# Bucketed attention and a mixture of experts on one core: a new order for VectorE's finishing steps, GpSimd's early gathers and the first weight splits

## The chip, the cores and the metric

One core of a Trainium2 chip runs the whole program. TensorE (PE) does the matmuls, VectorE (DVE), ScalarE (ACT) and GpSimd (POOL) the elementwise work, SyncE (SP) issues most DMAs. Each engine takes its own instructions in one fixed order and waits on semaphores for the others. The metric is the device time in microseconds.

## The reference, cut to what matters

```
mask   = q_bucket[:, :, :, None] == k_bucket[:, :, None, :]     # 6 sign bits of q @ proj, k @ proj
scores = where(mask, q @ k.T / 8, -1e9);  attn = softmax(scores);  x = attn @ v    # 4 x 8 heads x 768 x 64
x      = x.transpose(0, 2, 1, 3).reshape(3072, 512)
logits = x @ w_gate + modality_bias[modality_id]
e_idx  = argmax(logits);  gate_w = softmax(logits)[e_idx]
out[e_idx == e] = gate_w * (relu(x @ w1[e]) @ w2[e])            # 8 experts, 512 -> 1024 -> 512
```

## The kernel before, in words

**Attention.** The 32 heads are worked off as 16 pairs of heads, i = 0 to 15, four pairs to a batch of 768 tokens. A pair has six steps, one for each block of 128 keys. In a step TensorE makes the scores of all queries against the block (`score`, L278 and L279), ScalarE takes the exponential (pb, L291 and L296), TensorE multiplies by the values (`weigh`, L316), and the exponentials are summed (sp, L299) for the row sums: on GpSimd, two adds a step, except that in pair 15 the second head's adds are on VectorE, which leaves GpSimd five adds there. The exponentials lie in a ring of four buffers, freed only when both the value matmuls and the adds have read them. Between the score parts TensorE makes the row maxima of pair i+1 (`maxp`, reduced by VectorE from PSUM at L224 and L230, result mx) and turns, signs and patterns of pair i+2: `signs` gives bits (VectorE, L195), the bits times a pattern matrix (TensorE, L205) give the bucket rows of the operands, `maxp_back` puts the maxima into a_0g, a_1g and lone (VectorE, L249 and L250).

PSUM has two buffers for the maxima (psm) and two for transposes, patterns and the small products (psx).

**Finishing a batch.** Once a batch's four pairs are through, its outputs are finished beside the next batch's pairs, one generator step at a time (`finish`): row sums gs, reciprocals rin (L369 to L373), gate logits gl and lg (L377, L380), and `route`, which on VectorE makes the softmax and the argmax (l, rd, rw, oh, L567 to L580), the rank of each token in its expert (rk, run, pos, L595 to L601), and scatters records into a table with indirect DMAs on GpSimd (L605). For the last batches `finish_last` first runs `early_slots`: once two batches are routed it gives the two early expert slots their experts (L616 to L655, some 20 small VectorE operations on 128 x 8 to 128 x 96 elements: sg, enb, sc, ecu, ecux, sel, selx, selr, eslot, selw, early), and `early_tables` loads their token lists.

**Experts.** Two early slots, then the late ones, run as gathers of 512 token rows (xg, L766, four indirect DMAs on GpSimd), transposes, and matmuls in three products of high and low halves (L795 to L797, L839 to L841). Weights come in as raw and are split: ScalarE casts the high half (L749), the low half is a subtraction (L751) on VectorE or GpSimd: `pool = n % 2 == 1 if n < CFG["pn"]`.

**What sets the order.** TensorE and SyncE run in the order in which the code issues. For attention that is PLAN, one string for each of the six steps: S a score part, M a part of the maxima, T a piece for pair i+2, A values, B `maxp_back`, Q the row sums of the pair before, and the lower letters and G, F, E steps of finishing, which FIN gives to the pairs of a batch. VectorE, ScalarE and GpSimd are ordered by a scheduler when the program is built, from dependences and estimated costs; `tc.issue_after(ins)` puts what is issued in it behind the instruction ins on the same engine, an order only, with no semaphore.

## Time and profile before

| | |
|---|---|
| median of 3 runs | 827.99 us (827.86 to 829.27) |
| the profiled execution | 831.15 us, its span 829.4 us |
| mean granted TensorE clock | 0.974 |
| busy: TensorE, VectorE, ScalarE, GpSimd | 775.1, 490.8, 435.4, 448.4 us |

The profile is one execution, taken by the hardware profiler; all times in it count from the span's start. L195 is line 195 of the kernel before. In the changed file the same lines stand one to five lines lower from L23 on, some in `route` by other amounts. A timeline row gives start and length of an instruction, then in square brackets how long its engine was idle before it and what ended that wait. [...]

### The profile page before, as it was taken

To read this page: it belongs to the slowest core of one execution; us is meant where nothing else is said; L and a number is where in the kernel's file an instruction comes from. 1 tells how busy PE (TensorE), PEld (TensorE's weight loads), DVE (VectorE), ACT (ScalarE), POOL (GpSimd) and SP (SyncE) were. 2 spreads that over 40 slices of the span, in tenths; PEclk is the share of its full clock that TensorE was granted. 3 is DMA by queue.
4 is the path that set the end of the run, shared out by engine and by line. 5 is a ranking of instruction groups with operands and counts; after the bars stand their busy time and mean duration, and the time that the engine had idled before them with its cause. 6 is when DMAs were issued, how large, how long until landed. Compare 5 with 4: busy or idle time off the path is not lost. (4 is left out here: it accounts for less than half of the span.)

```text
span 829.4 us, 12179 instructions
## 1 busy us (share of the span) xinstructions
PE 775.1 (93%) x4252; PEld 548.5 (66%) x4252; DVE 490.8 (59%) x856; ACT 435.4 (52%) x788; POOL 448.4 (54%) x330
## 2 busy tenths in 40 slices
PE   5799999999999999999989898999999999999992
PEld 3556656565665665666556655888888888888882
DVE  5766767668886669776786656664344244643420
ACT  4477767666666666647655455333243335534340
POOL 5197788768769966859877976043220203302011
PEclk9699999999999999999998999999999999999996
DMA  9673446435545632743443327345543436733411
GB/s 205 141 169 97 96 115 152 104 70 134 148 101 134 152 94 74 178 129 63 115 115 95 123 82 185 131 98 187 161 125 107 146 103 204 268 102 118 124 49 36
DMA packets 105159, 104.27 MB, mean 126 GB/s; under 512 B 59389, under 2 KB 80509, under 8 KB 105088
## 3 DMA queue, kind: packets, MB, share of 16 engines
q1 hardware_dynamic: 98992, 88.61, 41.6%
q0 software_dynamic: 4928, 13.14, 4.5%
q10 hardware_dynamic: 1168, 1.64, 0.6%
q8 instruction: 36, 0.59, 0.3%
q14 instruction: 35, 0.29, 0.1%
HBM read 59.88 MB, written 13.33 MB: 88 GB/s over the span
## 5 line engine op out<-in xcount | busy, mean ns | idle before, releaser
L299 POOL TENSOR_TENSOR sp<-sp,pb 128x768 f32<-128x768 f32 x124 | 226.7, 1860 | 7.1 <-ACT pb L296 7.0
L291 ACT ACTIVATE pb<-pss 128x512 f32<-128x512 f32 x192 | 114.0, 602 | 101.0 <-PE pss L279 93.4
L224 DVE TENSOR_REDUCE mx<-psm 128x1 f32<-128x512 f32 x192 | 130.2, 686 | 30.3 <-PE psm L222 28.2
L316 PE MATMUL psu<-pb,vt 128*64 128x512 f32 (+1 forms) x768 | 134.2, 492 | 0.0
L751 DVE TENSOR_TENSOR w<-raw,w 128x1024 fp32r<-128x1024 f32 x60 | 75.5, 1260 | 96.8 <-ACT w L749 91.6
L749 ACT CAST w<-raw 128x1024 fp32r<-128x1024 f32 x64 | 67.0, 1049 | 75.8 <-PE yps L841 65.7
L316 PEld LDWEIGHTS psu<-pb,vt 128*64 128x64 f32 x768 | 51.0, 136 | 69.1 <-issue 58.8
L278 PE MATMUL pss<-a_0g 128*128 128x512 f32 x192 | 80.7, 420 | 4.9 <-ACT pb L291 4.2
L299 POOL TENSOR_TENSOR sp<-pb,pb 128x768 f32<-128x768 f32 x31 | 57.1, 1862 | 48.0 <-ACT pb L296 47.8
L839 PE MATMUL yps<-w,hl 128*128 128x512 f32 x208 | 82.6, 397 | 0.0
L841 PE MATMUL yps<-w,hh 128*128 128x512 f32 x208 | 81.3, 391 | 0.0
L840 PE MATMUL yps<-w,hh 128*128 128x512 f32 x208 | 81.0, 389 | 0.0
L795 PE MATMUL hps<-xh,w 128*128 128x512 f32 x192 | 76.7, 399 | 3.0 <-DVE hl L802 3.0
L797 PE MATMUL hps<-xh,w 128*128 128x512 f32 x192 | 76.1, 396 | 0.0
L796 PE MATMUL hps<-xl,w 128*128 128x512 f32 x192 | 76.1, 396 | 0.0
L278 PE MATMUL pss<-a_1g 128*128 128x512 f32 x192 | 70.7, 368 | 3.7 <-ACT pb L296 3.7
L230 DVE TENSOR_REDUCE mx<-psm 128x2 f32<-128x512 f32 x96 | 66.1, 689 | 9.6 <-PE psm L228 8.7
L766 POOL DMA_INDIRECT xg<-x_d,tb x18 | 22.1, 1227 | 91.8 <-DMA tb<-tab 87.5
L849 POOL DMA_INDIRECT out<-y,tb x18 | 19.1, 1059 | 95.2 <-ACT y L848 44.9
L801 ACT ACTIVATE hh<-hps 128x512 fp32r<-128x512 f32 x48 | 28.6, 597 | 79.5 <-PE hps L797 79.5
L279 PE MATMUL pss<-b_0g 128*128 128x512 f32 x192 | 66.3, 345 | 0.0
L279 PE MATMUL pss<-b_1g 128*128 128x512 f32 x192 | 66.2, 345 | 0.0
(210 smaller groups left out, 1484.1 us busy)
## 6 DMA issues: line engine op xcount, KB each, us to landing
raw<-moe_w SPq DMA_DIRECT2D x64, 512.0 KB
qk<-q SPq DMA_DIRECT2D x32, 192.0 KB
qk<-k SPq DMA_DIRECT2D x32, 192.0 KB
vt<-v SPq DMA_DIRECT2D x16, 384.0 KB
a_0g<-hx SPq DMA_DIRECT2D x30, 192.0 KB
a_1g<-hx SPq DMA_DIRECT2D x30, 192.0 KB
b_1g<-hx SPq DMA_DIRECT2D x30, 192.0 KB
b_0g<-hx SPq DMA_DIRECT2D x30, 192.0 KB
```

The lines of the kernel that those rows point to most:

```text
L224: nc.vector.tensor_reduce(out=mx[:, qt + j, 1 - h, 0:1], in_=mp, axis=AX.X, op=ALU.max)
L278: nc.tensor.matmul(out, t["s1"][h][:, ks], t["m1"][h][:, cs], start=True, stop=False)
L279: nc.tensor.matmul(out, t["s2"][h][:, ks], t["m2"][h][:, cs], start=False, stop=True)
L291: nc.scalar.activation(pb[:, h, 0:MAIN], sp, AF.Exp, scale=0.125)
L299: add = (nc.vector if h and i in CFG["spd"] else nc.gpsimd).tensor_tensor(out=t["sp"][:, h], in0=(t["pb"][0] if kt == 1 else t["sp"])[:, h ...
L316: nc.tensor.matmul(t["u"][part][64 * h:64 * h + 64, 0:w], t["v"][:, h, kt], t["pb"][kt][:, h, COLS[part]], start=False, stop=(kt == NT - 1 ...
L795: nc.tensor.matmul(hps, lo[:, c, fs], xh[:, c], start=(c == 0), stop=False)
L796: nc.tensor.matmul(hps, hi[:, c, fs], xl[:, c], start=False, stop=False)
L797: nc.tensor.matmul(hps, hi[:, c, fs], xh[:, c], start=False, stop=(c == 3))
L839: nc.tensor.matmul(yps[g], hl[fc][:, gs], hi[:, fb], start=(fc == 0), stop=False)
L840: nc.tensor.matmul(yps[g], hh[fc][:, gs], lo[:, fb], start=False, stop=False)
L841: nc.tensor.matmul(yps[g], hh[fc][:, gs], hi[:, fb], start=False, stop=(fc == 7))
```

## The change

Five edits. (1) The newest maximum reduction on VectorE is remembered, and every step of finishing is issued behind it. (2) In `route` the ranks rk and run move ahead of the softmax sum, with one more yield, and `finish_last` skips four places at step 12 instead of 11. (3) One G of PLAN moves from the last step of a pair to the third: two copies of gate values move earlier on TensorE in pairs 4 and 8. (4) The gathers of the early slots are issued on GpSimd behind named adds, counted from the last add of all. (5) `pn` goes from 8 to 0, so that all first splits are on VectorE.

```diff
+GAT = ((-5, -4, -4, -3), (-1, -1, -1, -1))
 PLAN = (
...
-    "SMTSMSMlEfxyk",
+    "SMTSMSMlGEfxyk",
...
-    "SMTSMTSMBAAFGBGFfFfggehkk",
+    "SMTSMTSMBAAFBGFfFfggehkk",
...
                     with tc.high_priority(offset=CFG["hm"]):
-                        nc.vector.tensor_reduce(out=mx[:, qt + j, 1 - h, 0:1], in_=mp, axis=AX.X, op=ALU.max)
+                        newest[:] = [nc.vector.tensor_reduce(out=mx[:, qt + j, 1 - h, 0:1], in_=mp, axis=AX.X, op=ALU.max).ins]
...
                     if add.ins.engine == mybir.EngineType.Pool:
                         latest[:] = [add.ins]
+                        adds.append(add.ins)
...
-            if n == 11:
+            if n == 12:
                 for _ in range(4):
                     yield
...
                     elif c in FIN[i >= NPR - 4][i % 4]:
-                        next(fins, None)
+                        with tc.issue_after(newest[0]):
+                            next(fins, None)
...
+        rk = wk.tile([P, NT, E], F32, name="rk")
+        nc.vector.tensor_tensor(out=rk, in0=pp[:, 0:NT * E].rearrange("p (t e) -> p t e", e=E), in1=run[b % 2].unsqueeze(1).broadcast_to([P, NT, E]), op=ALU.add)
+        nc.vector.tensor_tensor(out=run[(b + 1) % 2], in0=run[b % 2], in1=pp[:, 64:64 + E], op=ALU.add)
+        yield
         rec = recs[:, b]
         sm = wk.tile([P, NT], F32, name="rsum")
...
         for g in range(n):
-            nc.gpsimd.indirect_dma_start(out=xg[:, g], out_offset=None, in_=src, in_offset=bass.IndirectOffsetOnAxis(ap=at[:, g, 0:1], axis=0))
+            with tc.issue_after(adds[GAT[s[1]][g]]) if s[0] == "e" else nullcontext():
+                nc.gpsimd.indirect_dma_start(out=xg[:, g], out_offset=None, in_=src, in_offset=bass.IndirectOffsetOnAxis(ap=at[:, g, 0:1], axis=0))
```

Where this moves instructions is seen in the order that the build gives to each engine. The first place is VectorE in pair 12, before: maxima (mx), the sign operand b_1g, then bits.

```order
L224 TENSOR_REDUCE mx<-psm 128x1
L230 TENSOR_REDUCE mx<-psm 128x2
L224 TENSOR_REDUCE mx<-psm 128x1
L165 TENSOR_TENSOR b_1g_117<-psx,hx 128x512
L224 TENSOR_REDUCE mx<-psm 128x1
L230 TENSOR_REDUCE mx<-psm 128x2
L238 TENSOR_REDUCE m_4358<-mx 128x8
L195 TENSOR_SCALAR bits_164<-psx 128x384
```

The same place after the change; sg and enb stand some rows earlier among the maxima.

```order
L627 TENSOR_TENSOR sc_4386<-klow,enb 128x64
L239 TENSOR_REDUCE m_4362<-mx 128x8
L669 MEMSET ezero 128x8
L629 TENSOR_REDUCE ecu<-sc_4386 128x8
L631 TENSOR_TENSOR ecux<-ecu,enb 128x8
L638 TENSOR_TENSOR sel_4394<-ecu,kslot 128x16
L640 TENSOR_TENSOR selx_4396<-ecux,kslot 128x16
L641 TENSOR_TENSOR sel_4394<-sel_4394,selx_4396 128x16
L642 TENSOR_TENSOR selx_4396<-sel_4394,ke_66 128x16
L644 TENSOR_REDUCE selr_4400<-selx_4396 128x2
L645 CAST eslot<-selr_4400 128x2
L196 TENSOR_SCALAR bits_164<-psx 128x384
```

The first half of the early slots' chain now stands between the maxima of pair 12 and bits; before it stood in pair 11 ahead of gs (L339). Its second half, selw to selx, now stands behind the first lone of pair 12, ahead of the second a_0g.

The second place is VectorE in pair 13, before: the gate logits and the argmax of the third batch, then bits.

```order
L377 TENSOR_TENSOR gl<-gn,rin 128x384
L238 TENSOR_REDUCE m_4719<-mx 128x8
L380 TENSOR_REDUCE lg<-gl 128x48
L567 TENSOR_TENSOR l<-lg,bias 128x48
L569 TENSOR_REDUCE rm<-l 128x6
L571 TENSOR_TENSOR rd<-l,rm 128x48
L576 SCALAR_TENSOR_TENSOR rw<-rd,ke_66 128x48
L578 TENSOR_REDUCE rwm<-rw 128x6
L590 TENSOR_REDUCE rsum<-rex 128x6
L580 TENSOR_TENSOR oh<-rw,rwm 128x48
L591 TENSOR_SCALAR rsum<-rsum 128x6
L195 TENSOR_SCALAR bits_165<-psx 128x384
```

After the change, from the last maxima ahead of bits on.

```order
L231 TENSOR_REDUCE mx<-psm 128x2
L239 TENSOR_REDUCE m_4719<-mx 128x8
L196 TENSOR_SCALAR bits_165<-psx 128x384
L225 TENSOR_REDUCE mx<-psm 128x1 x2
L231 TENSOR_REDUCE mx<-psm 128x2
L374 SCALAR_TENSOR_TENSOR rin<-rin 128x48
L225 TENSOR_REDUCE mx<-psm 128x1
L375 RECIPROCAL rin<-rin 128x48
L225 TENSOR_REDUCE mx<-psm 128x1
L231 TENSOR_REDUCE mx<-psm 128x2
L250 SCALAR_TENSOR_TENSOR a_0g_114<-psx,a_0g_114 64x512
```

The chain from gl on is gone from ahead of bits: rin is among the maxima behind bits, gl comes behind the first lone, lg behind the second, and l to oh stand among the first maxima of pair 14.

The third place is GpSimd in the last pair, before: row scatters (L605), adds (L299), then the first splits (L751). Ahead of it, before the first add of pair 14, stood the eight gathers (L766).

```order
L605 DMA tab<-recs,posi 25088x2
L299 TENSOR_TENSOR sp<-pb_170,pb_171 128x768
L605 DMA tab<-recs,posi 25088x2
L299 TENSOR_TENSOR sp<-sp,pb_168 128x768
L605 DMA tab<-recs,posi 25088x2
L299 TENSOR_TENSOR sp<-sp,pb_169 128x768
L605 DMA tab<-recs,posi 25088x2 x2
L299 TENSOR_TENSOR sp<-sp,pb_170 128x768
L605 DMA tab<-recs,posi 25088x2
L299 TENSOR_TENSOR sp<-sp,pb_171 128x768
L751 TENSOR_TENSOR w<-raw,w 128x1024 x4
```

After the change, from the same first add of the last pair on.

```order
L300 TENSOR_TENSOR sp<-pb_170,pb_171 128x768
L609 DMA tab<-recs,posi 25088x2
L771 DMA xg<-x_d,ete 128x512
L300 TENSOR_TENSOR sp<-sp,pb_168 128x768
L609 DMA tab<-recs,posi 25088x2
L771 DMA xg<-x_d,ete 128x512 x2
L300 TENSOR_TENSOR sp<-sp,pb_169 128x768
L609 DMA tab<-recs,posi 25088x2 x2
L771 DMA xg<-x_d,ete 128x512
L300 TENSOR_TENSOR sp<-sp,pb_170 128x768
L609 DMA tab<-recs,posi 25088x2 x2
L300 TENSOR_TENSOR sp<-sp,pb_171 128x768
```

Four of the eight gathers now stand between the adds of the last pair, with one more scatter among them, and the other four behind its last add; the splits are gone from here.

## Rows read from the trace of the kernel before

**Rows 1.** Page, part 1: busy us of each engine (share of the span) xinstructions.
```profile
PE 775.1 (93%) x4252; PEld 548.5 (66%) x4252; DVE 490.8 (59%) x856; ACT 435.4 (52%) x788; POOL 448.4 (54%) x330
```

**Rows 2.** Timeline, TensorE: start, us, instruction [idle before <-releaser]; the four longest gaps.
```profile
362.48 0.79 PE L154 MATMUL psx<-ident,qk 128*128 128x128 f32 x4 [1.88 <-DVE gs L339]
...
435.59 0.48 PE L205 MATMUL psx<-bits,pat 128*128 128x384 bf16 x1 [3.29 <-DVE bits L195]
...
458.31 0.48 PE L278 MATMUL pss<-a_0g 128*128 128x256 f32 x1 [2.83 <-ACT pb L291]
...
514.23 0.47 PE L795 MATMUL hps<-xh,w 128*128 128x512 f32 x1 [3.03 <-DVE hl L802]
```

**Rows 3.** Windows: busy us of PE, PEld, DVE, ACT, POOL; granted clock; DMA; GB/s.
```profile
362.00:368.00 6.00, 5.52 (x27) 4.96 (x27) 4.81 (x8) 2.86 (x6) 2.60 (x2) 0.72 0.60 152
434.00:442.00 8.00, 6.41 (x27) 5.11 (x27) 5.08 (x13) 6.33 (x13) 4.47 (x4) 0.57 0.06 15
458.00:462.00 4.00, 3.69 (x25) 3.40 (x26) 2.81 (x6) 1.34 (x3) 3.56 (x3) 0.57 0.27 93
514.00:518.00 4.00, 3.77 (x17) 3.10 (x18) 2.07 (x6) 0.75 (x2) 2.40 (x1) 1.00 0.77 252
```

**Rows 4.** Timeline, GpSimd and VectorE: early-slot steps of pair 11 beside two adds.
```profile
356.37 3.67 POOL L299 TENSOR_TENSOR sp<-pb,pb 128x768 f32<-128x768 f32 x2 [5.26 <-ACT pb L296]
...
358.16 1.91 DVE L634 TENSOR_TENSOR sel<-ecu,kslot 128x16 f32<-128x16 f32 x1
...
360.00 0.17 DVE L636 TENSOR_TENSOR selx<-ecux,kslot 128x16 f32<-128x16 f32 x1
```

**Rows 5.** Timeline, GpSimd and VectorE: finishing steps of pair 13 ahead of bits.
```profile
425.38 7.54 POOL L299 TENSOR_TENSOR sp<-sp,pb 128x768 f32<-128x768 f32 x4
...
429.45 1.76 DVE L377 TENSOR_TENSOR gl<-gn,rin 128x384 f32<-128x384 f32 x1
...
431.14 0.16 DVE L238 TENSOR_REDUCE m<-mx 128x8 f32<-128x16 f32 x1
...
431.25 0.94 DVE L380 TENSOR_REDUCE lg<-gl 128x48 f32<-128x384 f32 x1
...
432.22 0.76 DVE L567 TENSOR_TENSOR l<-lg,bias 128x48 f32<-128x48 f32 x1
...
434.99 0.55 DVE L195 TENSOR_SCALAR bits<-psx 128x384 bf16<-128x384 f32 x1
```

**Rows 6.** Timeline, GpSimd: the first of eight gathers, and the adds behind the last.
```profile
446.15 0.99 POOL L766 DMA_INDIRECT xg<-x_d,ete  x1
...
455.92 3.64 POOL L299 TENSOR_TENSOR sp<-pb,pb 128x768 f32<-128x768 f32 x2
```

**Rows 7.** Timeline, GpSimd and TensorE: pair 12 round the first pattern matmul.
```profile
394.21 1.83 POOL L173 TENSOR_TENSOR b_0g<-xt,hx 128x768 fp32r<-128x768 f32 x1 [0.82 <-ACT xt L166]
...
396.00 7.20 POOL L299 TENSOR_TENSOR sp<-sp,pb 128x768 f32<-128x768 f32 x4
...
403.16 1.00 POOL L256 TENSOR_TENSOR va<-vt 128x384 f32<-128x384 f32 x1
...
401.82 0.34 PE L205 MATMUL psx<-bits,pat 128*128 128x384 bf16 x1
```

**Rows 8.** Timeline, GpSimd, TensorE and VectorE: the end of the last pair.
```profile
486.45 1.86 POOL L299 TENSOR_TENSOR sp<-sp,pb 128x768 f32<-128x768 f32 x1 [2.52 <-ACT pb L296]
...
498.33 1.95 POOL L299 TENSOR_TENSOR sp<-sp,pb 128x768 f32<-128x768 f32 x1
...
500.25 5.71 POOL L751 TENSOR_TENSOR w<-raw,w 128x1024 fp32r<-128x1024 f32 x2
...
500.45 0.85 PE L334 MATMUL psx<-sp,ones 128*32 128x384 f32 x8
...
511.40 2.08 DVE L751 TENSOR_TENSOR w<-raw,w 128x1024 fp32r<-128x1024 f32 x1 [2.70 <-ACT w L749]
```

**Rows 9.** Waits of TensorE: instruction <- releaser: us in total, times, longest us.
```profile
PE psm L228 <- DVE mx L224: 4.9, 7, 1.4
```

## The prediction

> **What bounds the kernel now.** I read the page first, then TensorE's timeline for its gaps, then the clock in windows round them, then the engine that each gap names. TensorE is busy 775.1 us, 93% of the span [rows 1], so only what lets it stand, or run slower, decides the time. After the start its longest gaps are four [rows 2]: C, 1.88 us at 362.48 behind gs; A, 3.29 us at 435.59 behind bits; B, 2.83 us at 458.31 behind an exponential; D, 3.03 us at 514.23 behind the low half hl of the first expert. The change touches the cause of all four. [...] Lost work by the windows: C 6 x 0.28 = 1.7 us; A 8 x 0.43 = 3.4 us, less up to 0.8 us that falls in the gap itself, so 2.9; B 4 x 0.43 = 1.7, less the gap's part, 1.6.

> Why VectorE was late: while GpSimd's adds run (3.67 us for two), the early slots' comparison sel, 16 elements a partition, takes 1.91 us and ends as the second add does; its twin selx behind it takes 0.17 us [rows 4]. In pair 13 gl takes 1.76 us inside a chain of adds, while reductions with one input, m and lg, take 0.16 and 0.94 us there, and the small l takes 0.76 us until the chain's end at 432.92 [rows 5]. I read this as: a VectorE step with two SBUF inputs waits out the GpSimd instruction that is running, one for each such step. So a chain costs by its number of such steps, where GpSimd is busy.

> **Removed.** C: the early slots' chain leaves pair 11, 1.9 + 1.7 = 3.6 us. A: the chain from gl on leaves the place ahead of bits, 3.3 + 2.9 = 6.2 us. B: eight gathers from 446.15 held the adds of pair 14 until 455.92 [rows 6], and through the ring of exponentials TensorE; they are moved past it, 2.8 + 1.6 = 4.4 us. Together 14.2 us. This is the surest term, 12.5 to 15.

> **Added in pair 12.** The early slots' first half now stands between the maxima and bits. sg meets b_0g on GpSimd, which runs until 396.04, and delays the reduction behind it: 0.7 us (0 to 1.5). Then sc, ecux, sel, selx, sel, selx: six steps with two SBUF inputs, behind which selr, eslot and bits are queued. GpSimd is occupied without a break from 396.00 on, by four adds of 1.8 us and the va chain at 403.16 [rows 7]. sc comes at about 397.9 and waits for the second add, to 399.6; ecux and sel for the third and fourth, to 403.2; the last three for the three va adds, to about 405.2. With the 0.7 us, and 0.9 us for selr, eslot and bits, plus starts, bits ends near 407.2. TensorE wanted it at 401.82 [rows 7], with the 0.7 at 402.5: a new gap of about 4.6 us. Ends: 0 if nothing is held, 7.8 us if each of the six waits 1.9. Gaps of 1.9 to 3.3 us cost 1.6 to 2.9 us of clock, so 2.4 more here (0 to 2.9). The second half, selw to selx, has four two-input steps between lone and the second a_0g, where TensorE's next pattern matmul waits for that a_0g's PSUM buffer: about one add's length, 1.8 us (0 to 3.5). Pair 12 in all: 0.7 + 4.6 + 2.4 + 1.8 = 9.5 us, between 0.5 and 15.

> **Added between pairs 13 and 14.** gl now stands between the first lone and the second a_0g, and lg behind the second lone: 1.76 + 0.94 = 2.7 us [rows 5] on VectorE where TensorE waits for these buffers, less some 0.5 us of slack: 2.2 (1 to 3.3). The steps l to oh follow among the maxima of pair 14, of which GpSimd has no add yet at its head; I cost them at nothing, and up to 1.9 us if one is held.

> **The other batches.** The same moves in pairs 5 to 7 and 9 to 11 put gl into the transition and take rk's tail out of the next. TensorE waits there for maxima 7 times, 4.9 us in all, 0.7 each [rows 9]; I let two such waits go and gain half a microsecond back in others: -0.8 us (-3 to +3). The G that moves in PLAN is work of the same length on TensorE: nothing.

> **The end.** GpSimd works from the second add of the last pair (486.45) to its last one without a long pause, ending at 500.28, and the row sums start on TensorE at 500.45 [rows 8]: no slack. Between those two adds there are now four more indirect DMAs, three gathers and a scatter. Eight gathers took 455.92 - 446.15 = 9.8 us, 1.22 each [rows 6], so 4.9 us; I take 4.3 of it as a wait of TensorE (3 to 6), since fewer splits and adds meet. Against it D goes: the splits on GpSimd took 5.71 / 2 = 2.86 us each [rows 8] and held raw buffers, and VectorE's split at 511.40, lengthened to 2.08 us, stood ahead of hl; with all of them on VectorE, and TensorE there later, I let the 3.0 us vanish. Net +1.3 (-3 to +6), with no clock term, as there was none after D.

> **Sum.** -14.2 + 9.5 + 2.2 - 0.8 + 1.3 = -2.0 us. The profiled execution, 831.15 us (span 829.4 and 1.75 us round it), would be 829.15. It lies 3.2 us above the median, so I apply the difference to that: 827.99 - 2.0 = 826.0 us. A measurement of this kernel can tell about 0.2% from no change, 1.7 us.

> **Rivals.**
> *The chain slips through.* In pair 11 sel was held for its add, and all that followed ran in 0.17 us each [rows 4]; if in pair 12 only one or two steps are held (the exponentials come later and GpSimd has pauses), the gap and its clock go, and pair 12 costs 3 us, not 9.5: -8.5 us, 819.5. Against it: GpSimd's 7.20 us of adds without a pause, just there [rows 7].
> *Every SBUF step of the chain is held* (slower). Then in pair 12 eslot's cast, two steps of early and one of selw wait too, four more GpSimd instructions of some 1.0 to 1.8 us: 9.5 becomes 15, the sum +3.5, 831.5 us. The place is VectorE ahead of bits and ahead of the second a_0g; it turns the change into a loss once pair 12 costs more than 11.5 us, and one that can be measured from 13.2 on. Against it: m and lg were not held [rows 5]. For it: no cast or scalar step from SBUF to SBUF stands beside an add in these rows.
> [...]
> *The end is dearer.* Four issues at 1.5 us rather than 1.22 make the wait 5.5 us, and a low clock behind it, as after C, A and B, costs up to 2.9: 1.2 + 2.9 more, the sum +2.1, 830.1 us. For it: the row sums have 0.17 us of slack. Against it: D's clock.

> **How the numbers follow.** Forecast 0.42 (alone 822 to 830), chain slips through 0.22, every step held 0.24, dearer end 0.12. Faster by over 0.2% (below 826.3): 0.55 of the first and all of the second, 0.23 + 0.22 = 0.45. Within 0.2%: 0.3 of the first and 0.04 from each of the last two, 0.21. Slower (above 829.7): 0.15 of the first, 0.20 and 0.08, 0.34. The range reaches from somewhat below the second case to beyond the third, 818 to 835.

> **What would show it.** Right: no gap at gs in pair 11, none at bits in pair 13, none at the exponentials of pair 14; a gap of 3 to 6 us at L206 in pair 12 with releaser bits, sel and selx of 1 to 1.9 us ahead of it and a clock of 0.5 after it; row sums at TensorE waiting 3 to 6 us for the last add; no gap behind hl. Wrong: sel and selx of 0.2 us in pair 12, or TensorE not waiting for bits there; the row sums not waiting, which would mean that the gathers fitted into pauses; or a new gap in pair 14, where the steps of the third batch now stand.

## The result and the profile after

The changed kernel takes 836.58 us (median of 4 runs, 836.02 to 837.56) against 827.92 for the kernel before: a ratio of 1.0103, with an interval of 1.0086 to 1.0121. It is slower by 8.7 us; the prediction had 826.0 and a range up to 835.0. The profiled execution took 836.02 us, its span is 834.2. TensorE is busy a little less than before, in a longer span [rows 1]:

```profile
PE 771.3 (92%) x4252; PEld 544.4 (65%) x4252; DVE 506.5 (61%) x860; ACT 436.0 (52%) x788; POOL 439.5 (53%) x326
```

What TensorE waited for is in its list of waits (instruction, releaser: us in total, times, longest); the line of [rows 9] has 16.1 us where it had 4.9.

```profile
PE psm L229 <- DVE mx L225: 16.1, 7, 10.0
```

Of the four gaps of [rows 2] none is left. Three new ones of more than 2 us stand in TensorE's timeline after the change, in pair 12, at the end of pair 12, and ahead of the row sums at the end:

```profile
401.14 0.80 PE L229 MATMUL psm<-a_1g 128*128 128x256 f32 x2 [10.02 <-DVE mx L225]
...
420.24 0.34 PE L206 MATMUL psx<-bits,pat 128*128 128x384 bf16 x1 [2.14 <-DVE lone L251]
...
507.37 1.51 PE L336 MATMUL psx<-sp,ones 128*32 128x384 f32 x8 [5.83 <-POOL sp L300]
```

The windows of the changed kernel (busy us of PE, PEld, DVE, ACT, POOL; granted clock; DMA; GB/s) give what [rows 3] gave of before: the granted clock, the share of TensorE's full clock that the profile gives for a stretch, is at or near 0.50 behind the first and the third gap.

```profile
392.00:400.00 8.00, 0.00 (x0) 0.00 (x0) 8.00 (x1) 0.00 (x0) 8.00 (x6) 0.70 0.82 191
400.00:404.00 4.00, 2.86 (x8) 1.46 (x10) 3.93 (x14) 1.22 (x2) 1.27 (x3) 0.50 0.24 54
404.00:408.00 4.00, 4.00 (x25) 1.64 (x21) 1.01 (x5) 0.00 (x0) 0.00 (x0) 0.83 0.43 94
506.00:510.00 4.00, 2.63 (x14) 1.20 (x15) 1.06 (x2) 0.00 (x0) 3.26 (x3) 0.50 1.42 365
510.00:512.00 2.00, 2.00 (x16) 1.83 (x19) 1.83 (x3) 1.64 (x3) 1.66 (x2) 0.70 0.53 47
```

The cause of the first gap is one step of VectorE. Here are VectorE and GpSimd in the changed kernel, pair 12, as [rows 7] had the same place before:

```profile
389.46 11.02 DVE L620 TENSOR_TENSOR sg<-run,kstep 128x96 f32<-128x96 f32 x1
...
403.46 0.17 DVE L631 TENSOR_TENSOR ecux<-ecu,enb 128x8 f32<-128x8 f32 x1
403.54 0.17 DVE L638 TENSOR_TENSOR sel<-ecu,kslot 128x16 f32<-128x16 f32 x1
...
385.91 0.96 POOL L609 DMA_INDIRECT tab<-recs,posi  x1 [0.30 <-issue]
386.89 3.72 POOL L300 TENSOR_TENSOR sp<-pb,pb 128x768 f32<-128x768 f32 x2
390.58 1.80 POOL L174 TENSOR_TENSOR b_0g<-xt,hx 128x768 fp32r<-128x768 f32 x1
392.35 7.06 POOL L300 TENSOR_TENSOR sp<-sp,pb 128x768 f32<-128x768 f32 x4
399.38 0.98 POOL L257 TENSOR_TENSOR va<-vt 128x384 f32<-128x384 f32 x1
400.44 0.45 POOL L258 TENSOR_TENSOR va<-va 128x128 f32<-128x128 f32 x1
```

sg, 0.25 us long in the kernel before (at 351.10), lasts 11.02 us: from 389.46 until the first pause of GpSimd, 400.36 to 400.44. It came beside the second add behind the scatter at 385.91, and six GpSimd instructions end in that time without letting it in. The maximum behind it, and with it TensorE, waits 10 us. The steps for which I had reckoned one hold each, ecux and sel among them, then take 0.17 us, because GpSimd has run out of adds until 411.27. The second gap belongs to the chain's second half, behind the first lone: there selw meets an add and is held for it.

```profile
416.80 1.75 DVE L652 SCALAR_TENSOR_TENSOR selw<-selw,ke 128x8 f32<-128x8 f32 x1
```

The change's gains are there as well. In pair 13 bits comes as soon as TensorE has its input, and gl, now in the transition, lasts 1.25 us:

```profile
440.19 0.56 DVE L196 TENSOR_SCALAR bits<-psx 128x384 bf16<-128x384 f32 x1 [2.60 <-PE psx L194]
...
448.63 1.25 DVE L379 TENSOR_TENSOR gl<-gn,rin 128x384 f32<-128x384 f32 x1
```

**Where the time went.** The profiled execution of before turned out to hold an event of its own (below), so I use a second profile of the kernel before, 828.35 us. The start of the same TensorE instruction in both, after less before, is -1.0 us at 355 us, -2.9 at 383, +11.7 at 411, +7.6 at 438, +5.8 at 466, +5.3 at 493, +8.1 at 520, and +7.9 at the end. So: pairs up to 10 gain 1.0, pair 11 gains 1.9, pair 12 loses 14.6, pair 13 gains 4.2, pair 14 gains 1.7 and pair 15 0.5, and the end loses 2.8 from 493 on. Of pair 12's loss 12.3 us come with the first gap and 2.3 with the second.

### The profile page after: what moved, and what is told of

Read it like the earlier page. It is cut to its first block, busy times and chain, and to the rows that moved or that the text cites. A ratio compares the mean times of both kernels' runs of the same rounds, so it can differ in the third digit from the quotient of the medians.

```text
span 834.2 us, 12174 instructions
## 1 busy us (share of the span) xinstructions
PE 771.3 (92%) x4252; PEld 544.4 (65%) x4252; DVE 506.5 (61%) x860; ACT 436.0 (52%) x788; POOL 439.5 (53%) x326
## 5 line engine op out<-in xcount | busy, mean ns | idle before, releaser
L300 POOL TENSOR_TENSOR sp<-sp,pb 128x768 f32<-128x768 f32 x124 | 224.8, 1845 | 11.6 <-ACT pb L297 11.5
L755 DVE TENSOR_TENSOR w<-raw,w 128x1024 fp32r<-128x1024 f32 x64 | 77.8, 1223 | 92.4 <-ACT w L753 91.7
L807 DVE SCALAR_TENSOR_TENSOR hl<-hps,hh 128x512 fp32r<-128x512 f32 x48 | 33.2, 691 | 55.5 <-ACT hh L806 55.5
```

The source lines that it names most:

```text
L300: add = (nc.vector if h and i in CFG["spd"] else nc.gpsimd).tensor_tensor(out=t["sp"][:, h], in0=(t["pb"][0] if kt == 1 else t["sp"])[:, h ...
L755: (nc.gpsimd if pool else nc.vector).tensor_tensor(out=lo, in0=r, in1=hi.bitcast(F32), op=ALU.subtract)
```

## The experiments

All times are medians; the ratio is to the kernel before on the same chip, whose median was 827.6 in the first four, 827.7 in the next four and 830.7 in h1 to h3.

### e1: the early slots' chain free of the newest maximum

```diff
-                        with tc.issue_after(newest[0]):
+                        early_step = i >= NPR - 4 and nslot[0] < 6
+                        nslot[0] += i >= NPR - 4
+                        with nullcontext() if early_step else tc.issue_after(newest[0]):
                             next(fins, None)
```

> The changed kernel, but the six steps of the early slots' chain are not issued behind the newest maximum; the scheduler puts the whole chain back into pair 11 ahead of gs, as in the kernel before. My theory: the change's loss of 8.7 us is one long hold of sg in pair 12 (+14.7 us there by the two profiles) and a wait at the end (+4.5), against 11.9 us of gains. Then the 14.7 go and the gap at gs comes back (+3.5): 836.6 - 11.2, about 825.4 us. Rival: a step with two SBUF inputs is held wherever it meets GpSimd's series of adds, so the price only moves with the chain: 834 to 837 us, with an equally long hold in pair 11.

827.01 us, ratio 0.9981 (0.9960 to 1.0002). Pair 12's 10 us gap is gone and the gap at gs is back with 2.0 us; against the changed kernel's profile it is 14.6 us better in pair 12, 12.3 of it at the first gap and 2.3 at the second, and 3.6 worse in pair 11. The theory holds, the rival falls: with the same sg in pair 11 TensorE's longest wait for a maximum is 1.4 us, where the changed kernel had 10.0.

### e2: the gathers at their old place

```diff
-            with tc.issue_after(adds[GAT[s[1]][g]]) if s[0] == "e" else nullcontext():
+            if True:
```

> The changed kernel, but the gathers of the early slots are issued without the named adds, so that the scheduler places them as before. My theory: the wait of the row sums at the end goes (it costs 7.5 us: 5.8 of gap and the low clock behind it, against which the 3.0 us gap behind hl had gone), the wait ahead of pair 14 comes back (+3.7): about 832.8 us. Rival: the end is bound by the weights in any case, and the gap behind hl comes back with the earlier start: 836 to 840 us.

833.21 us, ratio 1.0067 (1.0046 to 1.0088), near the number, but not by the reasons. The row sums still wait 2.0 us instead of 5.8, and the wait for exponentials at pair 14, gap B, did not come back: the longest there is 0.3 us. In its place another step was held, rk, directly behind the gathers:

```profile
465.83 4.29 DVE L601 TENSOR_TENSOR rk<-rk,oh 128x48 f32<-128x48 f32 x1
...
460.84 0.95 POOL L771 DMA_INDIRECT xg<-x_d,ete  x1 [0.30 <-issue]
461.81 3.69 POOL L300 TENSOR_TENSOR sp<-pb,pb 128x768 f32<-128x768 f32 x2
...
466.42 3.63 POOL L300 TENSOR_TENSOR sp<-sp,pb 128x768 f32<-128x768 f32 x2
```

rk lasts 4.29 us, over the ends of three GpSimd instructions, to the end of the adds in a series that begins with the last gather. By the profiles the gathers' old place costs 1.7 us in pair 14.

### f1: the gathers in GpSimd's pauses

```diff
-GAT = ((-5, -4, -4, -3), (-1, -1, -1, -1))
+GAT = ((-16, -16, -16, -6), (-6, -1, -1, -1))
```

> The changed kernel with the eight gathers behind other adds: three behind the last add of pair 13, two behind the last add of pair 14, three behind the last add of all; in the profile of the changed kernel GpSimd stands idle for 4.8 and 3.2 us at the first two places. My theory: they fit into the pauses, the row sums do not wait, 836.6 - 7.5 = 829 us with the long hold of sg still there. Rival: three gathers and what GpSimd owes are enough to delay the first adds of pair 14 or 15, and TensorE waits for exponentials again: 831 to 835 us.

833.80 us, ratio 1.0072 (1.0044 to 1.0100): 2.8 us better than the change, not 7.5. No exponential is waited for longer than 0.4 us, as the theory had it, but the row sums still wait 2.0 us: six scatters stand among the last pair's adds, where five stood in the kernel before; in the changed kernel one such scatter took 0.96 us (at 504.51) with 0.30 us ahead of it.

### p1: a probe ahead of sg

```diff
+        if row == 0:
+            nc.vector.tensor_tensor(out=g[:, 0], in0=slot[:, 0:12], in1=slot[:, 0:12], op=ALU.add)
         nc.vector.tensor_tensor(out=g, in0=cnt.unsqueeze(2).broadcast_to([P, E, 12]), in1=step[:, row], op=ALU.is_gt)
```

> The changed kernel with one VectorE step more, a sum of two SBUF operands of 12 elements a partition, just ahead of sg in pair 12 (its result is overwritten by sg). If the hold is a matter of the place (GpSimd's series of instructions that are all ready, not let go between them), the probe is held for some 9 to 11 us and sg takes 0.25 us. If it is a matter of sg's own form (96 elements, one operand broadcast), the probe is let in at the end of the GpSimd instruction that runs, under 1.9 us, and sg is held for the rest, 7 us or more.

One profile, 836.21 us. The probe, 12 elements a partition, lasts 10.90 us, and sg behind it 0.24:

```profile
389.52 10.90 DVE L621 TENSOR_TENSOR sg<-kslot 128x12 f32<-128x12 f32 x1
...
400.94 0.24 DVE L622 TENSOR_TENSOR sg<-run,kstep 128x96 f32<-128x96 f32 x1
```

So it is the place and not sg. In the traces so far a hold over several GpSimd instructions (sg 11.02 us, the probe 10.90, rk 4.29) stood only in a series that begins directly behind an indirect DMA; in pair 12 that is the scatter at 385.91. The next two runs take that away and put it elsewhere.

### q1: the scatters earlier

```diff
             scattered.append(ins)
-            if b < B - 1:
+            if b < B - 1 and (b != 1 or t < 3):
                 yield
+        if b == 1:
+            for _ in range(3):
+                yield
```

> The changed kernel with the last three row scatters of the second batch issued together, behind the last but one adds of pair 11, so that no indirect DMA of GpSimd stands directly ahead of the series of adds in which sg meets pair 12; VectorE's order is the same. In all traces so far a step is held over several GpSimd instructions only in a series that begins directly behind an indirect DMA (sg 11.0 us; in the run with the old gathers rk 4.3 us), and over one instruction in all other series. Theory: sg is then let in at the end of the instruction that runs, 1.9 us at most, the steps behind it are held for one instruction each, and pair 12 costs 5 to 9.5 us rather than 14.7: 828 to 832 us. Rival: the length of the series, or what VectorE did before, decides, and sg is held for 9 to 11 us again: 836 us.

830.34 us, ratio 1.0033 (1.0019 to 1.0047).

```profile
390.45 1.54 DVE L623 TENSOR_TENSOR sg<-run,kstep 128x96 f32<-128x96 f32 x1
...
394.47 1.08 DVE L630 TENSOR_TENSOR sc<-klow,enb 128x64 f32<-128x64 f32 x1
...
395.84 1.43 DVE L634 TENSOR_TENSOR ecux<-ecu,enb 128x8 f32<-128x8 f32 x1
...
397.30 1.79 DVE L643 TENSOR_TENSOR selx<-ecux,kslot 128x16 f32<-128x16 f32 x1
...
400.57 0.55 DVE L196 TENSOR_SCALAR bits<-psx 128x384 bf16<-128x384 f32 x1
...
390.04 1.84 POOL L174 TENSOR_TENSOR b_0g<-xt,hx 128x768 fp32r<-128x768 f32 x1 [0.36 <-ACT xt L167]
391.84 7.22 POOL L300 TENSOR_TENSOR sp<-sp,pb 128x768 f32<-128x768 f32 x4
```

With the scatters gone from ahead of the series, which now begins behind a pause of 0.36 us, sg is let in by the b_0g that runs, after 1.54 us. Further back in the same unbroken series sc, ecux and selx are held, 1.08, 1.43 and 1.79 us, one GpSimd instruction each; the sel between them slips through in 0.16 us. Bits is late, and TensorE waits 2.6 us for it. Pair 12 is 6.4 us better than with the change and costs 8.2 against the first profile of before. Of these 8.2, 1.9 are not the chain's: the moved scatters make the last add of pair 11 late, and the row sums at the head of pair 12 wait for it.

### q2: one scatter set into another series

```diff
                         adds.append(add.ins)
+                    if i == 13 and kt == 4 and h == 0:
+                        with tc.issue_after(add.ins):
+                            AGAIN[0]()
```

AGAIN holds one scatter of the second batch, issued a second time with the same rows; the base is e1.

> The kernel with the early slots' chain left free (827.0 us), with one scatter of the second batch issued a second time (same rows, same values) between the two adds of a step of pair 13, directly ahead of the adds among which gl comes; gl was held 1.26 us there, by one add. Theory (a series behind an indirect DMA lets VectorE in only at its first pause): gl takes 3 us or more, until the last add of pair 13 has ended. Rival: the indirect DMA is no cause, and gl is held for one add at most, under 1.9 us with its own time of 0.55.

One profile, 829.33 us. First gl in e1, then gl and GpSimd here:

```profile
439.17 1.26 DVE L379 TENSOR_TENSOR gl<-gn,rin 128x384 f32<-128x384 f32 x1
```

```profile
436.34 4.23 DVE L383 TENSOR_TENSOR gl<-gn,rin 128x384 f32<-128x384 f32 x1
...
433.76 0.99 POOL L615 DMA_INDIRECT tab<-recs,posi  x1 [0.15 <-issue]
434.77 5.37 POOL L301 TENSOR_TENSOR sp<-sp,pb 128x768 f32<-128x768 f32 x3
```

gl lasts 4.23 us instead of 1.26, until the last of the three adds behind the scatter has ended, at 440.14. TensorE's longest wait for the a_0g behind it is 2.7 us. The theory passes in both directions, each time in one profile.

### g1: both mends together

The edits of e1 and f1.

> The changed kernel with both mends: the early slots' chain free (827.0 us alone) and the gathers in GpSimd's pauses (2.8 us gained alone). Theory: the two add up, since they lie 90 us apart: 824.2 us, faster than the kernel before by some 3.4 us. Rival: the wait at the end is set by what reaches the last pair, and with TensorE there 10 us earlier the gathers' gain is lost: 827 us.

821.27 us, ratio 0.9909 (0.9890 to 0.9928): faster than both kernels, by more than I expected. By the profiles the gathers' move is worth 4.0 us at the end in f1, against the changed kernel, and 4.6 here, against e1; f1's profile came to the last pair 1.5 us later than the changed kernel's, for which I have no cause. Two waits of 2.0 us stay:

```profile
PE psx L336 <- POOL sp L300: 2.0, 1, 2.0
PE psx L155 <- DVE gs L341: 2.0, 1, 2.0
```

### e3 and h1: four of the first eight splits back on GpSimd

```diff
-CFG = dict(... pn=0, ...)
+CFG = dict(... pn=8, ...)
```

> The changed kernel with pn = 8: four of the first eight splits back on GpSimd. Theory: the gap behind hl (3.0 us before, none after the change) had its cause in these splits, 2.4 to 2.9 us each on GpSimd against 1.2 on VectorE, and now they would also queue behind the four gathers that follow the last add: 839.5 us or more. Rival: the gap went because TensorE starts the experts later, and the splits make no difference: 836 to 837 us.

e3, on the changed kernel: 842.85 us, ratio 1.0187 (1.0168 to 1.0207). h1 makes the same edit on g1:

> The kernel with both mends (821.3 us) with pn = 8, four of the first eight splits back on GpSimd. My theory: the gap behind hl is the price of these splits and comes back at 3 to 3.5 us; in the changed kernel they cost 6.3 us, where two steps of VectorE were also held behind gathers: 824 to 828 us. Rival: with the gathers mostly out of the way GpSimd has time for them, and nothing is lost: 821 us.

825.96 us, ratio 0.9948 (0.9928 to 0.9969), where g1 had 0.9909. The gap behind hl is back in both, first e3, then h1, there longer than the 3 to 3.5 us I expected:

```profile
523.73 0.47 PE L800 MATMUL hps<-xh,w 128*128 128x512 f32 x1 [3.47 <-DVE hl L807]
```

```profile
510.40 0.76 PE L802 MATMUL hps<-xh,w 128*128 128x512 f32 x1 [5.93 <-DVE hl L809]
```

So the fifth edit is a gain by itself: 0.8% on the changed kernel (1.0187 against 1.0103), and about 0.4% in g1, where the two intervals just meet. The two rivals fall.

### h2: g1 without the first edit

The diff is against g1.

```diff
-                        with nullcontext() if early_step else tc.issue_after(newest[0]):
+                        if True:
                             next(fins, None)
```

> The kernel with both mends without the first edit: no finishing step is issued behind the newest maximum, so VectorE's order there is the scheduler's, as in the kernel before. My theory: the gap ahead of bits in pair 13 (3.3 us and a low clock, 6 us by the profile of before, 4.8 by the two profiles) comes back, and small waits in pairs 5 to 10: 825 to 828 us. Rival: the first edit is worth nothing once sg is out of its reach, since it only exchanges one hold for another: 821 us.

824.50 us, ratio 0.9928 (0.9902 to 0.9954). The gap ahead of bits is back as it was, 3.30 us:

```profile
434.10 0.32 PE L206 MATMUL psx<-bits,pat 128*128 128x384 bf16 x1 [3.30 <-DVE bits L196]
```

The profile shows what the first edit removes (+4.9 us against g1 in pair 13, of which 2.7 come back, most of it in pairs 11 and 14); by the intervals, 0.9902 to 0.9954 and 0.9890 to 0.9928, a gain is likely but not shown.

### h3: the last add of the first head on VectorE

The base is g1. With one GpSimd add fewer, the places counted from the last add move by one.

```diff
-                    add = (nc.vector if h and i in CFG["spd"] else nc.gpsimd).tensor_tensor(
+                    add = (nc.vector if (h or kt == NT - 1) and i in CFG["spd"] else nc.gpsimd).tensor_tensor(
...
-GAT = ((-16, -16, -16, -6), (-6, -1, -1, -1))
+GAT = ((-15, -15, -15, -5), (-5, -1, -1, -1))
```

> The kernel with both mends, and the last add of the first head moved to VectorE as well, so that GpSimd has four adds in the last pair. My theory: the row sums' wait of 2.0 us at the end goes, with a low clock behind it of up to 1.5 us: 818 to 820 us. Rival: the chain of adds and scatters on GpSimd ends too late in any case (the last add waits for the one before it), and the wait stays: 821 us.

821.74 us, ratio 0.9897 (0.9862 to 0.9932), the same as g1. The row sums' wait went, and TensorE waits as long behind it, for the first expert's hl:

```profile
505.37 0.50 PE L802 MATMUL hps<-xh,w 128*128 128x512 f32 x1 [2.04 <-DVE hl L809]
```

### b0: the kernel before, profiled again

No edit.

> The kernel before, unchanged, profiled a second time. Its first profile, 831.15 us, lies 3.2 us above its median, and its gap B (2.83 us and a low clock, 4.4 us) shows VectorE and ScalarE both idle until 457.6 with a releaser called remote; with the gathers back at their old place B did not come back. Theory: B was a single event of that one execution; the second profile has gaps A, C and D and none at the exponentials of pair 14, and takes some 827 us. Rival: B belongs to the kernel, by the gathers ahead of pair 14 in its own order, and stands in the second profile too.

828.35 us. Gaps A, C and D stand as in [rows 2]; B does not:

```profile
361.76 0.66 PE L154 MATMUL psx<-ident,qk 128*128 128x128 f32 x4 [1.88 <-DVE gs L339]
...
433.28 0.48 PE L205 MATMUL psx<-bits,pat 128*128 128x384 bf16 x1 [3.30 <-DVE bits L195]
...
463.00 0.50 PE L228 MATMUL psm<-a_0g 128*128 128x256 f32 x2 [2.04 <-DVE mx L224]
...
510.13 0.47 PE L795 MATMUL hps<-xh,w 128*128 128x512 f32 x1 [3.17 <-DVE hl L802]
```

In its place is a wait of 2.04 us for a maximum, held up by rk behind the eight gathers:

```profile
456.57 5.27 DVE L597 TENSOR_TENSOR rk<-rk,oh 128x48 f32<-128x48 f32 x1
...
452.59 0.95 POOL L766 DMA_INDIRECT xg<-x_d,ete  x1 [0.30 <-issue]
453.56 3.69 POOL L299 TENSOR_TENSOR sp<-pb,pb 128x768 f32<-128x768 f32 x2
...
458.16 3.62 POOL L299 TENSOR_TENSOR sp<-sp,pb 128x768 f32<-128x768 f32 x2
```

B stands in only one of the two executions of the same kernel, the one that the prediction read. There, in the first profile of before, VectorE and ScalarE stood idle to the same moment:

```profile
457.56 0.56 DVE L339 TENSOR_TENSOR gs<-gs,psx 128x384 f32<-128x384 f32 x1 [5.96 <-remote]
...
457.66 1.09 ACT L291 ACTIVATE pb<-pss 128x512 f32<-128x512 f32 x2 [1.18 <-remote]
```

What they waited for the trace does not say. Without it, in the kernel before too, gathers directly ahead of adds cost a long hold, 5.27 us of rk, to the end of the adds at 461.78.

The clock behind the gaps differs between the two executions as well. Here are the windows behind C and D in the second profile; [rows 3] had 0.72 and 1.00.

```profile
361.00:367.00 6.00, 5.24 (x35) 4.62 (x35) 5.46 (x12) 4.05 (x8) 2.80 (x2) 1.00 0.56 149
510.00:514.00 4.00, 3.87 (x12) 3.09 (x13) 1.51 (x3) 0.21 (x1) 2.38 (x1) 0.68 0.80 247
```

## Why the prediction was wrong

**Removed.** Pairs 11 and 13 went as reckoned in place and cause: the chain left gs and bits free. Their sizes: 1.9 us for C against 3.6, since no low clock follows it in the second profile, and 4.2 for A against 6.2. The price of gl and lg, 2.2 in the sum, falls at the head of pair 14: TensorE waits 1.20 us for a maximum at 452.54, one of the signs of being wrong, and loses 1.4 there. B, 4.4 us, is missing from the second profile; by e2 the gathers' move gave 1.7 in pair 14. Reading a term off one gap of one execution failed there, and a sign was on the page: the profiled execution lay 3.2 us above its median, and the rows behind B name no instruction as the releaser.

**Pair 12, the step that failed.** "A VectorE step with two SBUF inputs waits out the GpSimd instruction that is running, one for each such step." The rows from which I took it showed only series that begin behind a pause or an add. In [rows 7] a pause of 0.82 us stood ahead of b_0g; in the changed kernel b_0g (390.58) follows the adds without a pause, in a series that begins behind a scatter (385.91). sg had 0.7 us in the sum, the hold by b_0g, and took 11.0 us: a wait of TensorE of 10.0 us and some 2 of clock behind it, 12.3 in all. The forecast's own bounds for pair 12 ended at 15, and 14.6 was measured, but sg alone is outside its bounds of 0 to 1.5, and the six steps ahead of bits cost TensorE nothing. The second half of the chain was right in place and cause, 2.3 against 1.8.

q1 shows how far the rule holds where no indirect DMA leads the series: a step is held for one instruction, but not every step is. Of the six ahead of bits four are held (the three above and the second sel, 0.92 us) and two take 0.16 and 0.17 us, as selx did behind sel in [rows 4], and the chain costs 6.3 us where 9.5 were forecast. The slower rival came near the size by luck: it had bits and the second a_0g late, not one step ahead of them. That a cast can be held, its premise, is true (below).

**The end.** The wait for the last add was 5.8 us, forecast 4.3 (3 to 6), and D went. I had taken no clock term since the clock held after D; after this gap it fell, 0.50 from 506 to 510, about 1.9 us of work lost from 507.4 to 512 ((510 - 507.4) x 0.50 + 2 x 0.30). The rival of a dearer end had both, 5.5 us and the clock. By the second profile the row sums cost 7.7 us and D's going gives back 4.9, more than its 3.2 us of gap, because there the clock behind D was low too. D's going is not due to TensorE's later start alone: h1 and e3 bring it back with the splits.

**The sum.** -2.0 was forecast; +8.1 is the sum of the stages by the second profile, +8.7 by the medians. Of the ten microseconds between, five are pair 12 (14.6 against 9.5), two are pairs 13 to 15 together (6.4 gained against 8.4, where B stood), and the rest are C's size and the end's, 1.7 and 1.5.

## What to carry to other kernels

## What the runs showed of the hardware

The hold behind an indirect DMA: sg 11.02 us in the changed kernel (TensorE's longest wait for a maximum is 10.0 us there, and in e2, f1 and e3 as well), the probe 10.90, rk 4.29 and 5.27, gl 4.23. sg, the probe and gl were held to the first pause of GpSimd (0.08 us at 400.36 for sg); rk was let in at the end of the last add, where a va step of GpSimd (0.44 us) follows without a visible pause, so what ends a hold is not fully shown. In all other series of the profiles of before and after, a step that was held was let in at the end of the GpSimd instruction that ran: sel of [rows 4] ends at 360.07, 0.03 us after its add, and in q1 sg at 391.99, 0.11 after b_0g. One case in the first profile of before looks like an exception: VectorE's split at 498.77 meets the add directly behind a scatter and is let in at that add's end, 500.28, though splits of GpSimd follow. But the trace has GpSimd's queue waiting for a semaphore there until 500.58, 0.3 us past the add, which reads as a pause; then the case fits. Why an indirect DMA has this effect was not tried and stays open.

A step with one SBUF input can be held too: the cast posi (6 elements) lasts 1.53 us beside an add in the changed kernel, against 0.16 in the kernel before, where no add ran:

```profile
239.27 1.53 DVE L605 CAST posi<-pos 128x6 int32<-128x6 f32 x1
...
237.12 3.65 POOL L300 TENSOR_TENSOR sp<-pb,pb 128x768 f32<-128x768 f32 x2 [4.54 <-ACT pb L297]
```
